# A fused attention and channel-mix kernel: the attention of the next batch issued between the matmul groups of the channel mix

## The chip, the cores and the metric

The kernel runs on one core of one Trainium2 chip. The core has five engines with a queue each: PE (matmuls and transposes, results into PSUM), ACT (activation functions), DVE (elementwise work), POOL and SP (here they mostly issue DMAs). An engine takes its own instructions in order and waits on semaphores for the others. The metric is the device time of one execution in microseconds (us), lower is better.

## The reference

Two stages, cut to what matters:

```python
# stage 1, per batch b and head h: B=8, H=8, S=576 tokens, D=64, M=32 memory slots
a   = softmax(phi, over the S tokens)          # [S, M]
k_m = a.T @ k ;  v_m = a.T @ v                 # [M, D] each
attn = softmax(q @ k_m.T / 8, over M)          # [S, M]
x[b, s, h*64:(h+1)*64] = attn @ v_m
# stage 2, on x [B, S, 512]; x_prev is x shifted by one token (0 for the first)
xk = mu_k*x + (1-mu_k)*x_prev ;  xr = mu_r*x + (1-mu_r)*x_prev
k  = maximum(xk @ w_k, 0)                      # [.., 1024]
out = sigmoid(xr @ w_r) * ((k*k) @ w_v)        # [B, S, 512], float32
```

All inputs and the output are float32; the kernel multiplies in bf16.

## The kernel before

Channels lie on the 128 partitions and tokens on the free axis in stage 2, so stage 1 has to leave x transposed (`xT`, `xk_T`, `xr_T`, each 128 x 4 x 4608).

Stage 1 is a loop over the eight batches (L90). A batch is cut into five token blocks of 128 (the last has 64). For each block, SP loads phi and POOL loads k, v and q with a cast to bf16 (L96, L102, L106, L156), one row of 64 values per token and head. ACT takes exp(phi) (L99). PE forms k_m (`psA`, L114), v_m for all pairs of heads (`psB`, L121) and the sums of exp(phi) (`psZ`, L126). DVE copies the blocks that are wanted out of PSUM (L136, L137, L148). PE transposes q (L161), DVE copies it out (L166). Then, for each of four pairs of heads, scores (`psc`, L170), exp on ACT (L175), the sums over M by a matmul with ones (`pzs`, L177), one over them as exp(-ln(z)) in two activations (L182, L183), the values (`pno`, L185) and their product with the reciprocal (L189). The three PSUM tiles of a pair share one buffer ("bigp"). DVE then makes the token difference and the two mixes (L194 to L201).

Stage 2 is a loop over nine chunks of 512 tokens (L209). Per chunk: eight groups of four matmuls for k (`pk`, L216), relu on ACT (L221) and square on DVE (L222); then, for each 128 tokens, eight matmuls (`pv`, L227), four (`pr`, L233), a sigmoid on ACT (L238), a product on DVE (L240) and the store by SP (L241). `pk`, `pv` and `pr` share two PSUM buffers ("mp"). A chunk is 80 matmuls of 512 columns.

The code writes stage 1 in full and then stage 2. The tile framework's scheduler sets the order on each engine, and it starts chunks of stage 2 as soon as their batches are there.

## Time and profile before

| | us |
|---|---|
| median of 3 runs | 418.77 |
| lowest and highest run | 416.33, 421.94 |
| span of the profiled execution, first to last instruction | 414.4 |
| busy in the span: PE, weight loads, DVE, ACT, POOL | 295.0, 118.8, 187.6, 270.4, 103.8 |
| 1392 matmuls, 505 DVE, 400 ACT instructions (table loads among them) | |
| DMA: 158471 packets, 31.23 MB written, of them 151792 under 512 bytes | |

For the profiled execution the span is the time that the profile gives; its own time with what lies around the span is not listed, and the three runs are 1.9 to 7.5 us above the span, the median 4.4 us.

How to read it: busy time is counted per engine, and the engines work beside each other. A matmul's busy time includes its way through the array, so matmuls in a row overlap; the cost of one in a row is the distance from start to start. "Granted clock" is the share of TensorE's 2.4 GHz that it was given: 1.00 is 2.4 GHz, 0.50 is 1.2 GHz; before the first record of the clock the views print 1.00, whatever it was.

### The profile page before, as it was taken

The numbers are of one execution on the slowest core, as the hardware profiler recorded it, in microseconds if no ns is written. First come the engines' busy times: TensorE is split into PE (matmuls) and PEld (weight loads), VectorE is DVE, ScalarE is ACT, GpSimd is POOL, SyncE is SP. The second block draws the span as 40 slices with busy tenths as digits, with TensorE's granted clock in tenths as the row PEclk, the third lists the DMA queues.
The fourth block names the chain that finished last, engine by engine and source line by source line (L and its number), as shares of the span: only waits on it lengthen the run. The fifth ranks groups of instructions, "written<-read, shape, count | busy, mean of one in ns | idle before, by whom it ended". The sixth has DMA issues, their size and how long they took to land.

```text
span 414.4 us, 4288 instructions
## 1 busy us (share of the span) xinstructions
PE 295.0 (71%) x1392; PEld 118.8 (29%) x1392; DVE 187.6 (45%) x505; ACT 270.4 (65%) x400; POOL 103.8 (25%) x129
## 2 busy tenths in 40 slices
PE   0055957876867698776877587467677888888884
PEld 0021322322232243323333232122223333333331
DVE  1004165647463666555756356564544232323231
ACT  1030487599998798999888888878994242423331
POOL 7244762560540263164053021010000000000000
PEclk9999999989896968878896999678898999999999
DMA  7999999892992399299289045130000101020101
GB/s 110 194 145 153 126 133 73 58 156 15 114 164 29 43 123 115 52 114 128 13 78 101 25 71 34 13 44 25 27 25 25 76 27 76 25 78 26 76 27 76
DMA packets 158471, 31.23 MB, mean 75 GB/s; under 512 B 151792, under 2 KB 153328, under 8 KB 158448
## 3 DMA queue, kind: packets, MB, share of 16 engines
q0 software_dynamic: 114608, 16.79, 59.3%
q1 hardware_dynamic: 43840, 14.17, 17.2%
q8 instruction: 11, 0.18, 0.2%
q14 instruction: 12, 0.10, 0.1%
HBM read 38.28 MB, written 9.44 MB: 115 GB/s over the span
## 4 chain that ended last, share of the span: by engine, by line
PE 30%; ACT 28%; issue 18%; DMA 15%; DVE 5%; POOL 4%; POOLq 0%; ACTq 0%; DVEq 0%
PE pv L227 11%; PE pk L216 8%; DMA kt<-in_k_dram 6%; PE pr L233 5%; DMA qt<-in_q_dram 5%; ACT L182 4%; ACT rsb L238 4%; DMA vot<-in_v_dram 4%; ACT L183 4%; ACT zsb L183 3%; ACT zsb L182 3%; ACT L238 2%; ACT esc L175 2%; DVE xT L189 2%; ACT L175 2%
## 5 line engine op out<-in xcount | busy, mean ns | idle before, releaser
L227 PE MATMUL pv<-wv,sqT 128*128 128x512 bf16 x288 | 79.8, 415 | 16.0 <-ACT rsb L238 16.0
L216 PE MATMUL pk<-xkT,wk 128*128 128x512 bf16 x288 | 79.4, 410 | 10.9 <-ACT rsb L238 5.4
L156 POOL DMA_DIRECT2D qt<-in_q_dram x40 | 33.6, 841 | 126.4 <-PE pqT L161 105.3
L189 DVE TENSOR_TENSOR xT<-pno,zsb 128x576 bf16<-128x576 f32 x32 | 24.2, 758 | 71.8 <-ACT zsb L183 64.5
L221 ACT ACTIVATE relu<-pk 128x512 bf16<-128x512 f32 x72 | 41.4, 591 | 23.0 <-PE pk L216 19.9
L238 ACT ACTIVATE rsb<-pr 128x512 f32<-128x512 f32 x36 | 21.5, 597 | 53.5 <-PE pr L233 53.4
L240 DVE TENSOR_TENSOR osb<-rsb,pv 128x512 f32<-128x512 f32 x36 | 24.6, 683 | 65.9 <-ACT rsb L238 64.8
L227 PEld LDWEIGHTS <-sqT 128*128 128x128 bf16 x288 | 29.3, 104 | 56.4 <-issue 30.7
L233 PE MATMUL pr<-wr,xrT 128*128 128x512 bf16 x144 | 42.5, 399 | 3.2 <-ACT relu L221 3.2
L175 ACT ACTIVATE esc<-psc,rZ1s 64x576 bf16<-64x576 f32 x32 | 23.5, 733 | 29.9 <-PE psc L172 29.7
L102 POOL DMA_DIRECT2D kt<-in_k_dram x40 | 34.1, 857 | 33.0 <-PE psA L114 24.0
L182 ACT ACT_TABLE_LOAD x32 | 41.1, 1283 | 0.6
L216 PEld LDWEIGHTS <-wk 128*128 128x128 bf16 x288 | 26.6, 101 | 43.9 <-issue 22.8
L222 DVE TENSOR_TENSOR sqT<-relu 128x512 bf16<-128x512 bf16 x72 | 29.6, 421 | 19.9 <-ACT relu L221 19.8
L106 POOL DMA_DIRECT2D vot<-in_v_dram x40 | 33.8, 850 | 12.4 <-PE psZ L126 5.0
L121 PE MATMUL psB<-vot,ephi 128*128 128x512 bf16 (+1 forms) x80 | 31.1, 498 | 5.8 <-DMA vot<-in_v_dram 5.2
L183 ACT ACT_TABLE_LOAD x26 | 33.4, 1283 | 0.5
L99 ACT ACTIVATE ephi<-phit 128x256 bf16<-128x256 f32 (+1 forms) x40 | 15.4, 409 | 27.6 <-DMA phit<-in_phi_dram 25.1
L170 PE MATMUL psc<-qTb,kmT 128*64 128x512 bf16 x32 | 15.2, 476 | 17.7 <-DVE xT L189 17.6
L114 PE MATMUL psA<-ephi,kt 128*128 128x128 bf16 (+1 forms) x160 | 20.5, 278 | 9.8 <-DMA kt<-in_k_dram 5.2
L197 DVE SCALAR_TENSOR_TENSOR xkT<-diff,mk,xT 128x576 bf16<-128x576 bf16 x32 | 25.9, 808 | 0.4
L201 DVE SCALAR_TENSOR_TENSOR xrT<-diff,mr,xT 128x576 bf16<-128x576 bf16 x32 | 25.9, 810 | 0.0
(48 smaller groups left out, 318.0 us busy)
## 6 DMA issues: line engine op xcount, KB each, us to landing
out_dram<-osb SPq DMA_DIRECT2D x36, 256.0 KB, 2.0
kt<-in_k_dram POOLq DMA_DIRECT2D x32, 128.0 KB, 5.6
vot<-in_v_dram POOLq DMA_DIRECT2D x32, 128.0 KB, 5.8
phit<-in_phi_dram SPq DMA_DIRECT2D x32, 128.0 KB, 5.7
qt<-in_q_dram POOLq DMA_DIRECT2D x32, 128.0 KB, 3.4
wk<-in_moe_w_k_dram POOLq DMA_DIRECT2D x1, 1024.0 KB, 9.2
wv<-in_moe_w_v_dram POOLq DMA_DIRECT2D x1, 1024.0 KB, 13.3
wr<-in_moe_w_r_dram POOLq DMA_DIRECT2D x1, 512.0 KB, 15.2
```

What stands on the lines that cost most here:

```text
L102: nc.gpsimd.dma_start(out=kt[:sn, :, :], in_=k[b, :, s0:s0 + sn, :].rearrange("h s d -> s h d"))
L106: nc.gpsimd.dma_start(out=vot[:sn, :H * D].rearrange("p (h d) -> p h d", h=H), in_=v[b, :, s0:s0 + sn, :].rearrange("h s d -> s h d"))
L156: nc.gpsimd.dma_start(out=qt[:sn, :, :], in_=q[b, :, s0:s0 + sn, :].rearrange("h s d -> s h d"))
L175: nc.scalar.activation(e_sc, psc, AF.Exp, scale=rZ1s[:, j:j + 1])
L182: nc.scalar.activation(zs_sb, pzs, AF.Ln)
L183: nc.scalar.activation(zs_sb, zs_sb, AF.Exp, scale=-1.0)
L189: nc.vector.tensor_mul(xT[:, j, b * S:(b + 1) * S], pno, zs_sb)
L216: nc.tensor.matmul(pk, lhsT=wk_sb[:, di, fi * 128:(fi + 1) * 128], rhs=xk_T[:, di, tok_sl], start=(di == 0), stop=(di == ND - 1))
L221: nc.scalar.activation(relu_t, pk[:, :], AF.Relu)
L227: nc.tensor.matmul(pv, lhsT=sq_T[:, fi, tsub * 128:(tsub + 1) * 128], rhs=wv_sb[:, fi, :], start=(fi == 0), stop=(fi == NF - 1))
L233: nc.tensor.matmul(pr, lhsT=xr_T[:, di, t0:t0 + 128], rhs=wr_sb[:, di, :], start=(di == 0), stop=(di == ND - 1))
L238: nc.scalar.activation(r_sb, pr[:, :], AF.Sigmoid)
```

## The change

The kernel is written anew around the same matmuls of stage 2. Stage 1 of batch b+1 becomes a list of steps, each with a slot number; a chunk of stage 2 has 16 slots (eight `key`, then `gate` and `value` mixed), and the program issues slot after slot, first the stage-2 group, then the steps of that slot. The scheduler is off (`manual_schedule`), so this order is the order on every engine. Steps of batch 0, and the first ones of batch 1, come ahead of slot 0.

Other parts: a batch's first 512 tokens are loaded as four tokens per partition (one run of 256 values of a head where there were four of 64) and the last 64 apart, two batches ahead; token columns are kept in that order through stage 2, and `store` puts rows back. k_m and v_m of a pair of heads come from one matmul with 64 weight columns and 256 moving columns, times a mask that clears the cross terms. The denominators are 48 rows of 96 columns for the whole batch (`zsum`), inverted by one reciprocal on DVE, split in two bf16 parts and spread again by matmuls (`spread`). exp of ln is gone. The gate is 0.5 + 0.5 tanh(x/2), with the 0.5 folded into w_v; the +1 is in the last product. All stage-1 PSUM tiles share three buffers ("at"); `pk` has two, `pr` and `pv` share three.

The diff, cut; the lines taken away are those of the loops listed above:

```diff
+NB = 4
+TAIL = 512
...
+    ctx.enter_context(tc.manual_schedule())
+    const = ctx.enter_context(tc.sbuf_pool(name="const", bufs=1))
+    big = ctx.enter_context(tc.sbuf_pool(name="big", bufs=1))
+    ld = ctx.enter_context(tc.sbuf_pool(name="ld", bufs=2))
+    work = ctx.enter_context(tc.sbuf_pool(name="work", bufs=2))
+    psum = ctx.enter_context(tc.psum_pool(name="psum", bufs=1))
...
+    def load_kv(b):
+        kvm = ld.tile([128, 2, H, NB, D], BF16, name="kvm", tag="kvm")
+        kvt = ld.tile([NT, 2, H, D], BF16, name="kvt", tag="kvt")
+        for i, t in enumerate((k, v)):
+            nc.gpsimd.dma_start(
+                out=kvm[:, i].rearrange("p h j d -> p h (j d)"),
+                in_=t[b, :, 0:TAIL, :].rearrange("h (p j) d -> p h (j d)", j=NB))
+            nc.gpsimd.dma_start(out=kvt[:, i], in_=t[b, :, TAIL:S, :].rearrange("h s d -> s h d"))
+        loads[b].update(kvm=kvm, kvt=kvt)
...
+    load_phi(0)
+    load_kv(0)
+    load_q(0)
+    mu2 = const.tile([2 * ND, 128], F32, name="mu2")
+    nc.sync.dma_start(out=mu2[:ND, :], in_=moe_mu_k.rearrange("(a b) -> a b", b=128))
+    nc.sync.dma_start(out=mu2[ND:2 * ND, :], in_=moe_mu_r.rearrange("(a b) -> a b", b=128))
+    load_phi(1)
+    wk_sb = big.tile([128, ND, Dff], BF16, name="wk")
+    wv_sb = big.tile([128, NF, Dm], BF16, name="wv")
+    wr_sb = big.tile([128, ND, Dm], BF16, name="wr")
+    nc.gpsimd.dma_start(out=wk_sb, in_=moe_w_k.rearrange("(do di) f -> di do f", di=128))
+    nc.gpsimd.dma_start(out=wr_sb, in_=moe_w_r.rearrange("(do di) d2 -> di do d2", di=128))
+    nc.gpsimd.dma_start(out=wv_sb, in_=moe_w_v.rearrange("(fo fi) d -> fi fo d", fi=128))
+    load_kv(1)
+    load_q(1)
+    identity = const.tile([128, 128], BF16, name="identity")
+    make_identity(nc, identity)
...
+        def exp_phi():
+            em = work.tile([128, NB, H, M], BF16, name="em", tag="em")
+            et = work.tile([NT, H, M], BF16, name="et", tag="et")
+            nc.scalar.activation(em.rearrange("p j h m -> p h j m"), L["phm"], AF.Exp)
+            nc.scalar.activation(et, L["pht"], AF.Exp)
+            st["em"] = em.rearrange("p j h m -> p j (h m)")
+            st["et"] = et.rearrange("p h m -> p (h m)")
+            if b + 2 < B:
+                load_phi(b + 2)
+                for j in blocks:
+                    last = j == NB
+                    n = NT if last else 128
+                    for c in range(2):
+                        for what in range(2):
+                            for jj in range(2):
+                                pr = 2 * c + jj
+                                e = st["et"][:, pr * 64:(pr + 1) * 64] if last else \
+                                    st["em"][:, j, pr * 64:(pr + 1) * 64]
+                                if what == 0:
+                                    rhs = L["kvt"][:, :, 2 * pr:2 * pr + 2, :] if last else \
+                                        L["kvm"][:, :, 2 * pr:2 * pr + 2, j, :]
+                                    o = st["kvps"][jj * 64:(jj + 1) * 64, c, :]
+                                else:
+                                    rhs = ones[:n, :]
+                                    o = st["zps"][jj * 64:(jj + 1) * 64, c:c + 1]
+                                nc.tensor.matmul(o, lhsT=e, rhs=rhs,
+                                                 start=(j == 0 and c == 0), stop=last,
+                                                 skip_group_check=True)
...
+        def norm_kv():
+            rz = work.tile([128, 2], F32, name="rz", tag="rz")
+            nc.vector.reciprocal(rz, st["zps"])
+            kvbd = work.tile([128, 2, 2, 2 * D], BF16, name="kvbd", tag="kvbd")
+            for c in range(2):
+                nc.vector.scalar_tensor_tensor(
+                    kvbd[:, c].rearrange("p a b -> p (a b)"), in0=st["kvps"][:, c, :],
+                    scalar=rz[:, c:c + 1], in1=mask.rearrange("p a h d -> p (a h d)"),
+                    op0=AL.mult, op1=AL.mult)
+            st["kvbd"] = kvbd
...
+        def tr_q(pr):
+            def go():
+                if "qT" not in st:
+                    st["qT"] = work.tile([128, NPAIR, S], BF16, name="qT", tag="qT")
+                ps = psum.tile([128, S], BF16, name="qtps", tag="at", bufs=3)
+                for j in range(NB):
+                    for i in range(2):
+                        nc.tensor.matmul(ps[i * D:(i + 1) * D, j * 128:(j + 1) * 128],
+                                         lhsT=L["qm"][:, 2 * pr + i, j, :], rhs=identity,
+                                         is_transpose=True, start=True, stop=True,
+                                         skip_group_check=True)
+                nc.tensor.matmul(ps[:, TAIL:S],
+                                 lhsT=L["qt"][:, 2 * pr:2 * pr + 2, :].rearrange("p h d -> p (h d)"),
+                                 rhs=identity[:NT, :NT], is_transpose=True, start=True, stop=True,
+                                 skip_group_check=True)
+                nc.vector.tensor_copy(st["qT"][:, pr, :], ps)
...
+        def scores(c, hf):
+            def go():
+                if "e" not in st:
+                    st["e"] = work.tile([128, 2, S], BF16, name="e", tag="e")
+                ps = psum.tile([128, HALF], F32, name="scps", tag="at", bufs=3)
+                sl = slice(hf * HALF, (hf + 1) * HALF)
+                for jj in range(2):
+                    nc.tensor.matmul(ps[jj * 64:(jj + 1) * 64, :],
+                                     lhsT=st["kmT"][:, c, jj * 64:(jj + 1) * 64],
+                                     rhs=st["qT"][:, 2 * c + jj, sl], start=True, stop=True,
+                                     skip_group_check=True)
+                nc.scalar.activation(st["e"][:, c, sl], ps, AF.Exp, scale=scale)
+            return go
+        def zsum():
+            ps = psum.tile([NROW, SEG], F32, name="zcps", tag="at", bufs=3)
+            for c in range(2):
+                for sg in range(NSEG):
+                    o = NROW - (c * 4 * NSEG + sg)
+                    nc.tensor.matmul(ps, lhsT=selz[:, o:o + NROW],
+                                     rhs=st["e"][:, c, sg * SEG:(sg + 1) * SEG],
+                                     start=(c == 0 and sg == 0), stop=(c == 1 and sg == NSEG - 1))
+            rzf = work.tile([NROW, SEG], F32, name="rzf", tag="rzf")
+            nc.vector.reciprocal(rzf, ps)
+            rhl = rhl2[b % 2]
+            nc.vector.tensor_copy(rhl[:NROW, :], rzf)
+            nc.vector.tensor_sub(rhl[LO:KR, :], rzf, rhl[:NROW, :])
+            st["rhl"] = rhl
+                n = HALF // SEG
+                for i in range(n):
+                    sg = hf * n + i
+                    nc.tensor.matmul(ps[:, i * SEG:(i + 1) * SEG],
+                                     lhsT=selb[:, c, sg].rearrange("p g m -> p (g m)"),
+                                     rhs=st["rhl"], start=(i == 0), stop=(i == n - 1),
+                                     skip_group_check=True)
+                sl = slice(hf * HALF, (hf + 1) * HALF)
+                nc.vector.tensor_mul(st["at"][:, c, sl], st["e"][:, c, sl], ps)
...
+                pss = [psum.tile([128, HALF], F32, name="nops", tag="at", bufs=3) for _ in range(2)]
+                for jj in range(2):
+                    r = slice(jj * 64, (jj + 1) * 64)
+                    nc.tensor.matmul(pss[jj], lhsT=st["kvbd"][r, c, 1, :],
+                                     rhs=st["at"][r, c, sl], start=True, stop=True,
+                                     skip_group_check=True)
+                for jj in range(2):
+                    nc.scalar.copy(st["x"][:, 2 * c + jj, sl], pss[jj])
...
+        def diff():
+            x = st["x"]
+            d = work.tile([128, ND, S], BF16, name="diff", tag="diff")
+            nc.vector.tensor_sub(d[:, :, 128:TAIL], x[:, :, 128:TAIL], x[:, :, 0:TAIL - 128])
+            nc.vector.tensor_sub(d[:, :, 1:128], x[:, :, 1:128], x[:, :, TAIL - 128:TAIL - 1])
+            nc.vector.tensor_copy(d[:, :, 0:1], x[:, :, 0:1])
+            nc.vector.tensor_sub(d[:, :, TAIL:S], x[:, :, TAIL:S], x[:, :, TAIL - 1:S - 1])
+            st["d"] = d
...
+        return [
+            (-9, exp_phi),
+            (-6, kv((0, 1))), (-5, kv((2, 3))), (-4, kv((4,))), (-4, norm_kv),
+            (-3, tr_q(0)), (-3, tr_q(1)), (-2, tr_k), (-1, tr_q(2)), (-1, tr_q(3)),
+            (0, scores(0, 0)), (1, scores(0, 1)), (2, scores(1, 0)), (3, scores(1, 1)),
+            (4, zsum),
+            (5, spread(0, 0)), (5, spread(0, 1)), (6, spread(1, 0)), (6, spread(1, 1)),
+            (7, values(0, 0)), (7, values(0, 1)), (8, values(1, 0)), (8, values(1, 1)),
+            (9, diff),
+            (10, mix(0, 0)), (10, mix(1, 0)), (11, mix(2, 0)), (11, mix(3, 0)),
+            (12, mix(0, 1)), (13, mix(1, 1)), (13, mix(2, 1)), (14, mix(3, 1)),
+        ]
...
+                nc.scalar.activation(th, pr, AF.Tanh, scale=0.5)
...
+                nc.vector.scalar_tensor_tensor(o, in0=st["pr"][ts], scalar=1.0, in1=pv,
+                                               op0=AL.add, op1=AL.mult)
...
+        return [key(fi) for fi in range(NF)] + [
+            gate(0), gate(1), value(0), gate(2), value(1), gate(3), value(2), value(3)]
...
+    slots = {}
+    for b in range(B):
+        base = 16 * (b - 1)
+        for rel in range(-9, 16):
+            slots.setdefault(base + rel, []).append((b, rel))
+    last = 16 * NCH
+    for s in range(-25, last):
+        mixing = channel_mix(s // 16) if s >= 0 and s % 16 == 0 else None
+        if mixing:
+            work_at["m"] = mixing
+        if s == 0:
+            nc.vector.tensor_scalar_mul(wv_sb.rearrange("p a b -> p (a b)"),
+                                        wv_sb.rearrange("p a b -> p (a b)"), 0.5)
+        if s >= 0:
+            work_at["m"][s % 16]()
+        for b, rel in slots.get(s, []):
+            for r, step in steps_of(b):
+                if r == rel:
+                    step()
```

POOL's queue at its start, before (a DMA row names its tile and the input, with what it waits for; the masks.py rows build the 128x128 identity that transposes need):

```order
masks.py:197 MEMSET identity 128x128
L74 DMA wk<-in_moe_w_k_dram 128x4x1024
masks.py:199 ISA
masks.py:199 AFFINE_SELECT identity<-identity 128x128 [waits Pool_49]
L75 DMA wv<-in_moe_w_v_dram 128x8x512
L76 DMA wr<-in_moe_w_r_dram 128x4x512
L102 DMA kt<-in_k_dram 128x8x64
L106 DMA vot<-in_v_dram 128x8x64
```

With the change, the same engine from the load of w_k on, which stands behind the six loads of batch 0:

```order
L102 DMA wk<-in_moe_w_k_dram 128x4x1024
L103 DMA wr<-in_moe_w_r_dram 128x4x512
L104 DMA wv<-in_moe_w_v_dram 128x8x512 [waits DMASW0_49]
L77 DMA kvm<-in_k_dram 128x8x256 [waits DMASW1_49]
L80 DMA kvt<-in_k_dram 64x8x64 [waits DMASW2_49]
L77 DMA kvm<-in_v_dram 128x8x256 [waits DMASW3_49]
L80 DMA kvt<-in_v_dram 64x8x64 [waits DMASW4_49]
L86 DMA qm<-in_q_dram 128x8x256 [waits DMASW5_49]
L89 DMA qt<-in_q_dram 64x8x64 [waits DMASW6_49]
masks.py:197 MEMSET identity 128x128
masks.py:199 ISA
masks.py:199 AFFINE_SELECT identity<-identity 128x128 [waits Pool_49]
```

The identity has moved from the head of the queue to behind all loads of two batches and the weights, and the last of these waits for an earlier load.

ACT in the middle of the kernel, before (a pair of heads of stage 1, `L182` and `L183`, with relu and sigmoid of stage 2 between):

```order
L183 ACT_TABLE_LOAD
L183 ACTIVATE zsb<-zsb 128x576
L221 ACTIVATE relu<-pk 128x512
L175 ACTIVATE esc<-psc,rZ1s 64x576
L182 ACT_TABLE_LOAD
L182 ACTIVATE zsb<-pzs 128x576
L183 ACT_TABLE_LOAD
L183 ACTIVATE zsb<-zsb 128x576
L238 ACT_TABLE_LOAD
L238 ACTIVATE rsb<-pr 128x512
L175 ACT_TABLE_LOAD
```

With the change, one period from the relu of slot 4 on (`e` is exp of the scores, `x` the copies of the attention's values, `em` and `et` the exp of the next phi, `th` the tanh of a gate):

```order
L358 ACTIVATE rl<-pk 128x512 [waits DVE_49,PE_49] x4
L292 CAST x<-nops 128x288 [waits PE_49] x4
L160 ACTIVATE em<-phm 128x8x4x32 [waits DMAHW0_49]
L161 ACTIVATE et<-pht 64x256 [waits DMAHW1_49]
L369 ACTIVATE th<-pr 128x512 [waits PE_49]
L292 CAST x<-nops 128x288 [waits PE_49] x4
L369 ACTIVATE th<-pr 128x512 [waits PE_49]
L369 ACTIVATE th<-pr 128x512 [waits DVE_49,PE_49,Activation_49]
```

The table loads between activations are gone. Four copies, the two exp of phi, a tanh and four more copies now stand in a row behind the relus of slots 4 to 7.

## Rows read from the trace of the kernel before

**Rows 1.** Stretch, length, busy us of PE, PEld, DVE, ACT, POOL; clock, DMA share, GB/s.

```profile
80.00:312.00 232.00, 168.94 (x825) 65.57 (x824) 130.62 (x348) 206.40 (x291) 63.36 (x76) 0.85 0.79 69
...
312.00:410.00 98.00, 84.89 (x372) 36.51 (x371) 29.94 (x59) 33.03 (x56) 0.00 (x0) 0.98 0.14 52
```

**Rows 2.** Groups by line, ACT: count, busy us, mean ns, idle before.

```profile
L221 ACT ACTIVATE relu<-pk 128x512 bf16<-128x512 f32 x72 | 41.4, 591 | 23.0 <-PE pk L216 19.9 <-DVE sqT L222 2.9
L182 ACT ACT_TABLE_LOAD x32 | 41.1, 1283 | 0.6
L183 ACT ACT_TABLE_LOAD x26 | 33.4, 1283 | 0.5
...
L238 ACT ACTIVATE rsb<-pr 128x512 f32<-128x512 f32 x36 | 21.5, 597 | 53.5 <-PE pr L233 53.4
...
L99 ACT ACTIVATE ephi<-phit 128x256 bf16<-128x256 f32 (+1 forms) x40 | 15.4, 409 | 27.6 <-DMA phit<-in_phi_dram 25.1 <-PE psB L121 2.3
```

**Rows 3.** Chain of waits from 325 us on: start us, us, work.

```profile
327.91 7.07 PE pk L216 x32
...
348.56 7.07 PE pk L216 x32
...
410.48 0.69 DVE osb L240
```

**Rows 4.** Busy time by stretch, as rows 1, in the loading at the start.

```profile
4.00:8.00 4.00, 0.00 (x0) 0.00 (x0) 0.00 (x0) 0.00 (x0) 4.00 (x6) 1.00 1.06 161
...
8.00:12.00 4.00, 0.00 (x0) 0.00 (x0) 0.17 (x1) 0.00 (x0) 1.41 (x2) 1.00 1.30 190
12.00:18.00 6.00, 0.00 (x0) 0.00 (x0) 0.19 (x4) 0.02 (x1) 0.87 (x1) 1.00 1.43 213
20.00:40.00 20.00, 10.05 (x51) 4.44 (x52) 4.42 (x22) 4.83 (x16) 8.39 (x10) 1.00 2.06 149
```

**Rows 5.** Timeline of PE at full clock: start us, us, instructions merged.

```profile
158.12 0.39 PE L114 MATMUL psA<-ephi,kt 128*128 128x128 bf16 x4
158.44 0.39 PE L185 MATMUL pno<-esc,vmx 64*128 64x512 bf16 x1
...
162.95 0.40 PE L170 MATMUL psc<-qTb,kmT 128*64 128x512 bf16 x1 [0.31 <-DVE xT L189]
163.19 0.19 PE L172 MATMUL psc<-qTb,kmT 128*64 128x64 bf16 x1
163.31 1.04 PE L233 MATMUL pr<-wr,xrT 128*128 128x512 bf16 x4
```

**Rows 6.** Timeline of PE, earlier in the run.

```profile
66.24 0.58 PE L170 MATMUL psc<-qTb,kmT 128*64 128x512 bf16 x1 [1.61 <-DVE xT L189]
66.62 0.26 PE L172 MATMUL psc<-qTb,kmT 128*64 128x64 bf16 x1
66.81 0.61 PE L114 MATMUL psA<-ephi,kt 128*128 128x128 bf16 x4
```

**Rows 7.** Groups by line, DVE.

```profile
L222 DVE TENSOR_TENSOR sqT<-relu 128x512 bf16<-128x512 bf16 x72 | 29.6, 421 | 19.9 <-ACT relu L221 19.8
...
L197 DVE SCALAR_TENSOR_TENSOR xkT<-diff,mk,xT 128x576 bf16<-128x576 bf16 x32 | 25.9, 808 | 0.4
L240 DVE TENSOR_TENSOR osb<-rsb,pv 128x512 f32<-128x512 f32 x36 | 24.6, 683 | 65.9 <-ACT rsb L238 64.8 <-ACT zsb L182 0.6 <-issue 0.4
L189 DVE TENSOR_TENSOR xT<-pno,zsb 128x576 bf16<-128x576 f32 x32 | 24.2, 758 | 71.8 <-ACT zsb L183 64.5 <-PE pno L187 7.3
...
L166 DVE COPY qTb<-pqT 128x512 bf16<-128x512 bf16 (+1 forms) x40 | 15.7, 393 | 17.9 <-PE pqT L161 16.4 <-PE psc L172 1.5
L194 DVE TENSOR_TENSOR diff<-xT 128x575 bf16<-128x575 bf16 x32 | 14.5, 452 | 0.3
```

**Rows 8.** Busy time by stretch, as rows 1, around one fall of the clock.

```profile
120.00:123.00 3.00, 1.67 (x8) 0.57 (x6) 2.24 (x8) 2.92 (x8) 0.26 (x1) 1.00 2.42 147
124.00:127.00 3.00, 2.29 (x9) 0.76 (x8) 0.82 (x2) 2.70 (x5) 0.00 (x0) 0.50 0.06 15
```

More of the change, by code (lines that the diff above doesn't have):

```diff
@@ new lines @@
+    load_kv(1)
+    load_q(1)
+    identity = const.tile([128, 128], BF16, name="identity")
+    make_identity(nc, identity)
+    ident_f = const.tile([2 * ND, 2 * ND], F32, name="identf")
+    nc.vector.tensor_copy(ident_f, identity[:2 * ND, :2 * ND])
+    ones = const.tile([128, 1], BF16, name="ones")
+    nc.vector.memset(ones, 1.0)
+    mask = const.tile([128, 2, 2, D], BF16, name="mask")
+    nc.vector.memset(mask, 0.0)
+    for g in range(4):
+        nc.vector.memset(mask[g * M:(g + 1) * M, :, g % 2, :], 1.0)
```

329 lines of the change are left out of this document (146 added, 183 removed).

## The prediction

> **What bounds the kernel now.** I read the busy time by stage first. From 80 to 312 us ACT is busy 206.4 of 232 us, PE 168.9, DVE 130.6 and POOL 63.4; from 312 on PE alone is full, 84.9 of 98 us [rows 1]. So there are two stages: one in which attention and channel mix are mixed and ACT is the full engine, and one of channel mix alone. The costs by line say what fills ACT: the two largest of its table-load groups are 58 loads of 1.28 us, 74.5 us [rows 2], because Exp, Ln, Exp again and Sigmoid take turns. The chain of waits then gives the pure price of stage 2. One chunk takes 20.65 us from key group to key group; its 32 key matmuls take 7.07 us, 0.221 us each [rows 3]. Eighty of them are 17.7 us; the other 3 us are waits for the two shared buffers.
>
> The start is a third stage: the transfer rate by window is 161 GB/s (written) from 4 us, 190, then 213 while the weights come, and 149 from 20 us on, when the rows of 64 values come [rows 4].
>
> **What goes.** Ln, the second Exp, Sigmoid and with them all but one table load leave ACT. What stays there per chunk is 8 relus of 0.59 us, 4 tanh of 0.60 [rows 2] and per batch four exps and eight copies of 288 columns and two exps of phi. At 0.41 us for 256 columns and 0.59 for 512 [rows 2], 288 cost 0.43, and the 1024 of the larger exp of phi 0.95. That is 7.1 + 6.5 = 13.6 us a chunk, far under PE's work below. DVE per chunk: 8 squares of 0.42, 4 last products of 0.68, 8 mixes of 0.81, the difference at 0.45 per 575 columns (1.9), copies of 0.39 to 0.47 (2.2 in all), four products of 288 columns at half of 0.76 (1.6), and an estimated 1.7 for the normalizations, small operations at these rates: 20 us [rows 7]. Also under PE. So PE should set the time from the first key group to the end, if its waits are small, and I sum its queue.
>
> **1. Ahead of the first key group: 60 us.** In the new order PE's first instruction, and DVE's, need the identity, and POOL makes it only behind the last load of batch 1, which waits for `wk`. Ahead of that land batch 0 (2.36 MB as written), the phi of batch 1 (0.59) and `wk` (1.05), 4.0 MB. From 4 to 12 us the windows give 1.4 MB [rows 4]. For the rest no row has runs of 512 bytes written. Bounds are 149 GB/s (runs of 128 bytes) and 213 (1 to 2 KB) [rows 4]; a straight line of time per run through the two, 13.7 and 96 ns per DMA engine, gives 41 ns for 512 bytes, 199 GB/s, and I take that: 12 + 2.6/0.199 = 25 us (24 to 29), and 27 with POOL's last issue and the identity itself.
>
> From there the first batch runs alone, step behind step, and PE at half clock, as before at this point: 576 columns in two matmuls take from 66.24 to 66.81, 0.57 us, where later they take 0.36 [rows 5, 6]. Twenty matmuls of 256 columns at 0.25 and twenty small ones: 6.2, to 33.5. Normalization on DVE 1.2, then transposes at 0.13 [rows 6], nine per pair of heads, held by three buffers: 38.7. Scores 8 x 0.28: 40.9. Exp, sums, reciprocal, spread and product: 44. Then eight copies of 0.43 on ACT with the exp of the next phi (1.36) among them: 49.3. Difference 1.9 and five mixes of 0.81 on DVE: 55.2. Only then DVE normalizes batch 1 (1.1), does two mixes and two copies (2.6), and PE, done with batch 1's k and v long before, can end the last two groups of transposes: 60. The loads of batch 1 (7.3 MB by then, about 42 us) lie beside this and are not late. At full clock the PE pieces would give back about 8 us.
>
> **2. A chunk with attention beside it: 31.2 us, six times.** Key, gate and value groups: 17.7. The attention steps of a batch at full clock: a matmul of 128 columns in a row costs 0.08 (four from 158.12 to 158.44) [rows 5], so 34 transposes and four short ones 3.0, and 24 of 96 columns 1.9; 20 of 256 columns at half of 0.221, 2.2; 16 of 288, 2.0; 20 of one column at an estimated 0.06 (between nothing and the 0.08), 1.2. Sum 10.3. Each visit to matmuls with 64 weight columns or rows costs some more: 576 columns from 162.95 to 163.31 are 0.36 us, 0.11 over 576 columns at the full-width rate [rows 5, 3]; 14 visits, 1.5. Upper end 11.8. The lower end is that two neighbouring 64-wide matmuls, now on different halves of the array, run side by side: half of 2.2 + 2.6 + 2.0 comes off, 8.4. The rows have 64-wide matmuls only on the first half, so none is nearer to either end; I take the middle, 10.1.
>
> The Trainium skill (TensorEngine Tiling (Array Packing), section Key Properties) has a rule for each end: different tiles work in parallel, and a change of tiling mode drains the array. The drain agrees with the 0.11 us of the row; the parallel part no row shows, and by it the sum would be that of the lower end.
>
> Then the waits. Behind key group 7, ACT has in a row a relu, four copies, two exp of phi, a tanh and four copies: 0.59 + 1.72 + 1.36 + 0.60 + 1.72 = 6.0 us [rows 2]. PE has two gate groups and eight value matmuls in that stretch, 2.8 us, and its value matmuls need buffers that these copies free: it waits 3.1. The reciprocals for `spread` come about 0.3 late. So 17.7 + 10.1 + 3.4 = 31.2, 187 us for six.
>
> **3. The rest.** Chunk 6 has only the second half of a batch beside it, and no exp of phi: 17.7 + 4.2 + 1.9 = 23.8. Chunks 7 and 8 have nothing beside them, and with three buffers for `pr` and `pv` no wait: 35.4. After the last value group follow a product of 0.69 and the store; before, 414.4 minus 410.48 is 3.9 [rows 3]: 4.0 with the hand-over.
>
> The loads of later batches (2.36 MB in 31 us) and the stores in smaller pieces lie beside this: the start moves more than twice that rate. Scaling `w_v` once on DVE (3 to 6 us by the rates of rows 7) lies beside the first key groups, whose buffers give it four relus' time. These cost nothing; without that cover the second is at most 6 us, once.
>
> **4. The clock.** Half clock follows stretches in which PE was little busy: 1.67 of 3 us from 120, then 0.50 from 124 [rows 8]. The new wait of step 2 makes one such stretch per chunk. If every second one is followed by a stretch at half clock like that in rows 8, 3 us at least, in which PE does half, it loses 0.75 us a chunk, 5 in all.
>
> Sum: 60 + 187 + 24 + 35 + 4 + 5 = 315 to 316 for the span, against 414.4. The runs' median is 4.4 above the span of before; with the same beside it **320 us**.
>
> **Rivals.**
> - *The pairs run side by side and the clock holds.* For it: the weights are put on both halves. Minus 11 and minus 5: **304**. Chance 0.25.
> - *The clock is granted as in the mixed stage of before*, 0.85 there [rows 1]. The interleaved PE work, about 189 us without waits, would lose 33 instead of 5: **348**. For it: stage 1's matmuls are short and thin here too. Against: PE was busy 73% of that stage, and would be near 88%. Chance 0.20.
> - *DVE's chain between copies and transposes sets the period.* Slots 0 to 7 of PE (10.5), ACT's 6.0, then difference, mixes, normalization, copies and last products one behind the other (14.5) and the last transposes (2.5) are 33.5 a chunk: **335**. Against: key groups and part of the gates run beside it. Chance 0.09.
> - *Slower than before: PE at half clock through the whole interleaved stage.* It loses 189 instead of 5: **504**. It decides from the point where 59% of that work (112 us lost) runs at half clock; the mean of 0.85 in rows 1 means that before it was under a fifth. Chance 0.03.
> - *The table loads do not go* (tanh and exp in different tables): at most 72 loads of 1.28, 92 us on an ACT with 200 us to spare, felt in the row of step 2 as two loads, 2.6 us a chunk: **338**. But the program of the changed kernel has one load. Chance 0.01.
>
> **How the numbers follow.** The forecast has 0.42; alone it would range from 306 to 338 (start 57 to 65, waits of 2 to 5 us a chunk). With the rivals at 304, 335 and 348 and the bounds of the start (8 us less at full clock, 5 more at 149 GB/s) the range is 292 to 362. About 2% (410 and 427) is what measurement can tell from no change. All cases but one lie under 410: faster 0.96; the half-clock case is spread over its degrees, 0.02 for within 2% and 0.02 for slower.
>
> **What would show it.** One table load; DVE's first instruction near 27 us; the first key group near 60; key group to key group 31 us for six chunks, with ACT's row of copies as the releaser of PE's waits on `nops`; 17.7 us for the last chunks; 64-wide pairs starting together or 0.11 apart; the granted clock of 60 to 275 us over 0.9. It would be wrong if PE waited for DVE or for loads in mid-kernel, or if the first key group came 15 us earlier or later.

## The result and the profile after

| | us |
|---|---|
| changed kernel, median of 4 runs | 293.61 (291.07 to 294.89) |
| kernel before, 4 runs on the same chip | 419.28 (416.33 to 421.94) |
| ratio, 95% interval | 0.7001 [0.6949, 0.7054]: faster |
| profiled execution of the changed kernel: its time, its span | 294.89, 293.1 |

Forecast 320 (292 to 362); the median lies 1.6 us inside the lower end. The profiled execution is the longest of the four; their spans go from 289.3 to 293.1, each 1.8 us below its time.

The chain of waits of the changed kernel gives the start of each chunk (start us, us, work). It answers to [rows 3].

```profile
54.31 1.82 PE pk L354 x4
...
84.60 0.97 PE pk L354 x4
...
114.71 0.97 PE pk L354 x4
...
143.16 0.97 PE pk L354 x4
...
253.61 6.91 PE pk L354 x32
270.88 6.91 PE pk L354 x32
...
288.24 0.69 DVE o L380
```

Key group to key group: 30.1 us, then 28.45, and 17.27 for the chunks with nothing beside them. The first key group comes at 54.3.

Busy time by stretch, columns as [rows 1]: the loading, a chunk with a fall of the clock, one without, and the last two chunks.

```profile
4.00:28.00 24.00, 0.41 (x3) 0.36 (x5) 0.48 (x5) 1.36 (x2) 9.65 (x14) 1.00 1.36 204
...
84.60:114.70 30.10, 27.82 (x199) 11.95 (x200) 18.55 (x40) 11.84 (x26) 4.70 (x6) 0.94 0.70 110
114.70:143.20 28.50, 26.21 (x200) 11.60 (x200) 17.93 (x39) 11.85 (x26) 4.70 (x6) 1.00 0.79 125
...
253.60:288.00 34.40, 34.40 (x161) 15.47 (x158) 13.07 (x26) 14.34 (x24) 0.00 (x0) 1.00 0.21 61
```

In the chunk without a fall (third row) PE is busy 26.2 of 28.5 us, ACT 11.9, DVE 17.9. Before, in the mixed stage, ACT was the full engine at 206 of 232 [rows 1]; now PE is, and its queue is what a chunk costs. The loads move at 204 GB/s in the loading stretch; [rows 4] gave 149 for short runs and 213 for long ones.

The groups by line, ACT (answers to [rows 2]), show where its time went.

```profile
L358 ACT ACTIVATE rl<-pk 128x512 bf16<-128x512 f32 x72 | 43.0, 597 | 88.1 <-PE pk L354 88.1
L369 ACT ACTIVATE th<-pr 128x512 f32<-128x512 f32 x36 | 21.5, 596 | 56.5 <-PE pr L366 53.7 <-DVE o L380 2.8
L292 ACT CAST x<-nops 128x288 bf16<-128x288 f32 x64 | 20.8, 413 | 3.8 <-PE nops L288 3.7
...
L160 ACT ACT_TABLE_LOAD x1 | 1.3, 1283 | 0.7 <-PEq L431 0.7
```

One table load is left. Relu and gate cost what they did.

### The profile page after: what moved, and what is told of

Its sections match the earlier page's. It is cut to its first block, busy times and chain, and to the rows that moved or that the text cites. A ratio compares the mean times of both kernels' runs of the same rounds, so it can differ in the third digit from the quotient of the medians.

```text
span 293.1 us, 4271 instructions
## 1 busy us (share of the span) xinstructions
PE 237.4 (81%) x1665; PEld 107.7 (37%) x1665; DVE 160.3 (55%) x351; ACT 104.1 (36%) x221; POOL 41.8 (14%) x57
## 4 chain that ended last, share of the span: by engine, by line
PE 68%; ACT 11%; DVE 9%; DMA 7%; POOL 2%; issue 1%; DVEq 0%; POOLq 0%
PE pv L377 22%; PE pk L354 21%; PE pr L366 10%; DMA wk<-in_moe_w_k_dram 7%; PE qtps L222 4%; ACT x L292 4%; PE kvps L188 3%; ACT rl L358 3%; PE scps L242 3%; ACT em L160 2%; DVE rzf L258 2%; PE rbps L272 2%; PE qtps L226 1%; ACT th L369 1%; DVE sq L359 1%
## 5 line engine op out<-in xcount | busy, mean ns | idle before, releaser
L358 ACT ACTIVATE rl<-pk 128x512 bf16<-128x512 f32 x72 | 43.0, 597 | 88.1 <-PE pk L354 88.1
L377 PE MATMUL pv<-wv,sq 128*128 128x512 bf16 x288 | 68.7, 385 | 0.0
L359 DVE TENSOR_TENSOR sq<-rl 128x512 bf16<-128x512 bf16 x72 | 30.6, 425 | 41.6 <-ACT rl L358 41.3
L369 ACT ACTIVATE th<-pr 128x512 f32<-128x512 f32 x36 | 21.5, 596 | 56.5 <-PE pr L366 53.7
L377 PEld LDWEIGHTS <-sq 128*128 128x128 bf16 x288 | 27.4, 99 | 32.2 <-issue 2.9
L380 DVE SCALAR_TENSOR_TENSOR o<-th,pv 128x512 f32<-128x512 f32 x36 | 24.6, 683 | 25.9 <-PE pv L377 22.3
L307 DVE SCALAR_TENSOR_TENSOR xrT<-diff,mu,x 128x576 bf16<-128x576 bf16 x32 | 25.2, 810 | 0.0
L288 PE MATMUL nops<-atn,kvbd 64*128 64x288 bf16 x64 | 15.1, 301 | 11.5 <-ACT x L292 9.6
L307 DVE SCALAR_TENSOR_TENSOR xkT<-diff,mu,x 128x576 bf16<-128x576 bf16 x32 | 24.0, 812 | 0.0
L292 ACT CAST x<-nops 128x288 bf16<-128x288 f32 x64 | 20.8, 413 | 3.8 <-PE nops L288 3.7
```

The lines of the kernel that those rows point to most:

```text
L288: nc.tensor.matmul(pss[jj], lhsT=st["kvbd"][r, c, 1, :], rhs=st["at"][r, c, sl], start=True, stop=True, skip_group_check=True)
L292: nc.scalar.copy(st["x"][:, 2 * c + jj, sl], pss[jj])
L307: nc.vector.scalar_tensor_tensor(dst[:, d4, b * S:(b + 1) * S], in0=st["d"][:, d4, :], scalar=mu1[:, which * ND + d4:which * ND + d4 + 1], ...
L358: nc.scalar.activation(rl, pk, AF.Relu)
L359: nc.vector.tensor_mul(st["sq"][:, fi, :], rl, rl)
L369: nc.scalar.activation(th, pr, AF.Tanh, scale=0.5)
```

## The experiments

Each ratio is to the kernel before, with its 95% interval. "The changed kernel" is the one above, whose lines the diffs start from, unless said otherwise.

### Do the two column halves run side by side?

**Program order of the pairs.** In `kv` and `tr_q` all matmuls of one half are written ahead of those of the other, where they alternated.

```diff
-                        for what in range(2):
-                            for jj in range(2):
+                        for jj in range(2):
+                            for what in range(2):
...
-                for j in range(NB):
-                    for i in range(2):
+                for i in range(2):
+                    for j in range(NB):
```

> The changed kernel with another order of the same matmuls: in the k/v step and in the transposes of q, the matmuls of one 64-column half follow one another and no longer alternate with those of the other half. Theory (the two halves of the array work side by side): in the changed kernel eight transposes of 128 columns start within 0.35 us and a pair of 256 columns plus a pair of one column takes 0.14 to 0.16; apart, a batch's k/v step goes from 1.6 to about 2.8 us and its transposes from 1.9 to 2.5 or 3, so six chunks grow by 1.7 to 2.4 us each and the first two batches, at half clock, by some 3 in all on the path: 305 to 312 us. Rival (the small price comes from the narrow weights alone, whatever the neighbour): 292 to 296 us, and the same start-to-start times.

Measured: 294.92, ratio 0.7038 [0.7000, 0.7076]; the changed kernel's 0.7001 lies in that interval. Expected were 305 to 312 if the halves run side by side, so this looked like evidence against it, and I read PE's timeline. The changed kernel:

```profile
103.61 0.30 PE L188 MATMUL kvps<-kvm,em 128*64 128x256 bf16 x2
103.74 0.17 PE L188 MATMUL zps<-ones,em 128*64 128x1 bf16 x2
103.77 0.28 PE L188 MATMUL kvps<-kvm,em 128*64 128x256 bf16 x2
...
109.06 0.41 PE L222 MATMUL qtps<-identity,qm 128*64 128x128 bf16 x8
109.41 0.20 PE L226 MATMUL qtps<-identity,qt 64*128 64x64 bf16 x1
```

And the reordered one, at the same step:

```profile
102.18 0.30 PE L188 MATMUL kvps<-kvm,em 128*64 128x256 bf16 x2
102.31 0.17 PE L188 MATMUL zps<-ones,em 128*64 128x1 bf16 x2
```

Both show the two halves' `kvps` together, then both `zps`. In the reordered program the order as written, with the scheduler off, is `kvps`, `zps` of one half and then `kvps`, `zps` of the other; single records start at 102.178 and 102.185 (`kvps`), 102.312 and 102.318 (`zps`). So the second `kvps` started 0.13 us ahead of a `zps` that stands before it in the program. The edit had not taken the pairs apart, and its result says nothing against them.

The Trainium skill (PSUM — Partial Sum Buffer, section Engine vs sequencer instructions) says that matmuls start and complete in program order. These records do not agree for matmuls on different column halves.

**A fence between the halves.** Half by half as above, with a matmul of one column over the full width ahead of each half; the tail's transpose, also of full width, stands between the halves of `tr_q`.

```diff
+                for jj in range(2):
+                    nc.tensor.matmul(st["zps"][:, 2:3], lhsT=identity, rhs=ones,
+                                     start=(jj == 0 and 0 in blocks), stop=False,
+                                     skip_group_check=True)
+                    for j in blocks:
...
+                    if i == 0:
+                        nc.tensor.matmul(ps[:, TAIL:S],
...
```

> The changed kernel with the two 64-column halves kept apart by a matmul of full width between them: in each k/v step all of one half, a one-column matmul with 128 weight columns, then all of the other half (five such fences more per batch than needed for the result); in the transposes of q the tail transpose, which has 128 weight columns, now stands between the halves. The run before this one only changed the order and the halves still started within 13 ns of each other. Theory (halves run side by side, and PE takes the other half's matmuls ahead of program order unless something of full width stands between): a batch's k/v step goes from 1.6 to 2.8 us or more and its transposes from 1.9 to 2.4 to 2.8 us, 1.7 to 2.3 us a chunk, at half clock twice that in the start: 304 to 311 us. Rival (narrow weights are cheap in themselves): at most the six fences a batch, 294 to 297 us.

Measured: 315.50, ratio 0.7507 [0.7466, 0.7549]. The same step in PE's timeline:

```profile
110.70 0.30 PE L191 MATMUL kvps<-kvm,em 128*64 128x256 bf16 x1
110.83 0.17 PE L191 MATMUL zps<-ones,em 128*64 128x1 bf16 x1
110.86 0.28 PE L191 MATMUL kvps<-kvm,em 128*64 128x256 bf16 x1
...
118.15 0.41 PE L225 MATMUL qtps<-identity,qm 128*64 128x128 bf16 x4
118.49 0.20 PE L230 MATMUL qtps<-identity,qt 64*128 64x64 bf16 x1
118.62 0.42 PE L225 MATMUL qtps<-identity,qm 128*64 128x128 bf16 x8
```

Four matmuls now come where eight did (`x4` from 118.15 to 118.49, against `x8` from 109.06 to 109.41): the side-by-side reading is shown. The last row shows the same within the run: between the tail transposes of two groups no fence stands, and there the second half of one group and the first half of the next, eight in all, again take 0.36 us. Per batch the k/v step takes 3.96 us where it took 1.70, two groups of transposes 1.30 instead of 0.96; a fence costs 0.10 of it, six times. The undisturbed chunk grew from 28.45 to 31.15. So 0.6 of the 2.7 us a chunk are the fences themselves. The run is 4.5 us above what was expected: a chunk grew by 2.7 where 1.7 to 2.3 was said, and the first key group comes 5.1 later (59.4), since the first batch's steps lie bare on the path. The two matmuls of a score step start together too (single records at 115.610 and 115.613 in the changed kernel), but what scores and values gain from it was not tried.

### ACT's row

**exp of phi one slot later,** behind the second four copies instead of between the two fours.

```diff
-            (-9, exp_phi),
+            (-8, exp_phi),
```

> The changed kernel with the two exp of the next batch's phi one slot later, behind the last four copies of the attention's values instead of ahead of the tanh of gate 0. Theory (ACT's row of relu, copies, exp and tanh is what PE waits for at the last value matmul, 1.3 us a chunk): the wait shrinks to about 0.5, the half-clock stretches behind it go, the first batch's chain loses 1.4 us of exp: 284 to 288 us, granted clock above 0.99. Rival (the wait only moves to the k/v step, which then waits for the exp, or to DVE's difference): 292 to 294 us.

Measured: 286.65, ratio 0.6843 [0.6805, 0.6881]. The changed kernel's ACT, one row of it:

```profile
95.70 1.30 ACT L292 CAST x<-nops 128x288 bf16<-128x288 f32 x4
96.85 1.10 ACT L160 ACTIVATE em<-phm 128x1024 bf16<-128x1024 f32 x1
97.81 0.42 ACT L161 ACTIVATE et<-pht 64x256 bf16<-64x256 f32 x1
98.11 0.59 ACT L369 ACTIVATE th<-pr 128x512 f32<-128x512 f32 x1
98.59 1.28 ACT L292 CAST x<-nops 128x288 bf16<-128x288 f32 x4
```

From the first copy to the last end it is 4.17 us. PE goes on before that end, when the first of the second four copies has freed a buffer:

```profile
99.04 0.28 PE L288 MATMUL nops<-atn,kvbd 64*128 64x288 bf16 x1 [1.30 <-ACT x L292]
```

PE's waits in the changed kernel (us in all, times, longest):

```profile
PE nops L288 <- ACT x L292: 9.6, 8, 1.3
PE rbps L272 <- DVE rhl L261: 6.6, 8, 1.4
...
PE nops L288 <- DVE atn L277: 1.1, 7, 0.2
```

and with the later exp:

```profile
PE nops L288 <- ACT x L292: 4.4, 7, 0.6
```

The wait on the copies halves, 1.30 to 0.62 a chunk, the period falls to 27.77, and the first key group comes 1.2 earlier. No stretch at half clock is left in mid-kernel. In the changed kernel the two falls begin at 99.2 and 157.3 us, within 0.4 of the end of this wait (99.0 and 157.6). They differ between executions: the mean clock of its four is 0.984 to 0.999, and 0.996 to 0.997 in the four with the later exp. Its windows around one fall, and at the same place of the next chunk:

```profile
96.00:99.00 3.00, 1.74 (x9) 0.43 (x9) 0.26 (x1) 3.00 (x9) 0.00 (x0) 1.00 0.02 5
99.00:102.00 3.00, 2.96 (x8) 1.04 (x8) 1.57 (x4) 1.47 (x4) 0.00 (x0) 0.54 0.73 195
126.10:129.10 3.00, 1.75 (x9) 0.45 (x9) 0.28 (x1) 3.00 (x9) 0.00 (x0) 1.00 0.00 0
```

PE was as little busy in the third stretch as in the first, and the clock held behind it. Why one fell and the other not stays open.

**Sigmoid again,** as a plain product and without the scaling of `w_v`; everything else as changed.

```diff
-                nc.scalar.activation(th, pr, AF.Tanh, scale=0.5)
+                nc.scalar.activation(th, pr, AF.Sigmoid)
...
-                nc.vector.scalar_tensor_tensor(o, in0=st["pr"][ts], scalar=1.0, in1=pv,
-                                               op0=AL.add, op1=AL.mult)
+                nc.vector.tensor_mul(o, st["pr"][ts], pv)
```

> The changed kernel with Sigmoid in place of Tanh, a plain product and no scaling of w_v: ACT then loads a table twice a chunk, 14 loads of 1.28 us instead of one. Theory (in the new order a load costs only where ACT's row is waited for: ahead of the first gate, inside the wait on the copies): 1.3 us in each of six chunks, some of it again as clock falls: 300 to 306 us. Rival (every load is on the path): 13 x 1.28, 310 us or more; other rival (ACT has room everywhere): 293 to 296.

Measured: 317.46, ratio 0.7556 [0.7511, 0.7601]; the time is the rival's, but not for its reason. From its waits, its ACT timeline and its windows:

```profile
PE nops L288 <- ACT x L292: 19.0, 8, 2.7
...
PE pk L354 <- ACT rl L358: 1.4, 6, 0.2
```

```profile
102.07 1.28 ACT L369 ACT_TABLE_LOAD   x1
```

```profile
121.00:152.80 31.80, 27.86 (x199) 12.03 (x199) 18.45 (x39) 14.45 (x28) 4.70 (x6) 0.95 0.67 107
```

Fourteen loads make 18.0 us, and the kernel is 23.9 longer. Two a chunk: one in the row, where PE's wait grows from 1.30 to 2.73, and one ahead of the first exp of the scores, where PE waits only 0.23. So one load of the two is on the path, as the theory had it, and PE waits 1.66 a chunk more. The rest is the clock, which the theory had too small: the chunks, 31.8 to 33.0 us, are 3.3 to 4.5 longer than 28.45, at a clock of 0.90 to 0.95.

### The start

**Identity early.** POOL makes it behind the loads of k and v of batch 0.

```diff
     load_kv(0)
+    identity = const.tile([128, 128], BF16, name="identity")
+    make_identity(nc, identity)
...
-    identity = const.tile([128, 128], BF16, name="identity")
-    make_identity(nc, identity)
```

> The changed kernel with the identity made behind the k and v loads of batch 0 instead of behind all loads. Theory (the identity's place in POOL's queue holds PE and DVE until 27.4 us): PE starts when batch 0's k and v are there (about 16.6 us), its transposes when q is there (about 21); from the first transpose to the first key group are 22.8 us in the changed kernel, so the first key group comes near 44 instead of 54.2: 283 to 285 us. Rival (the start is bound by the transfers of batch 1, whose last load lands near 36 to 38): first key group at 46 to 50, 288 to 290. If neither queue nor transfers matter: 293.6.

Measured: 289.64, ratio 0.6919 [0.6872, 0.6967]: the rival. The first batch's k/v matmuls start at 16.3 instead of 27.8, and then PE waits for the loads of the second, in its timeline:

```profile
41.61 0.42 PE L188 MATMUL kvps<-kvm,em 128*64 128x256 bf16 x2 [8.50 <-DMA kvm<-in_v_dram]
```

Of 11.5 us gained, 5.2 arrive at the first key group (49.1).

**Short runs.** Each large load of k, v and q as four, of 64 values a run.

```diff
-            nc.gpsimd.dma_start(
-                out=kvm[:, i].rearrange("p h j d -> p h (j d)"),
-                in_=t[b, :, 0:TAIL, :].rearrange("h (p j) d -> p h (j d)", j=NB))
+            for j in range(NB):
+                nc.gpsimd.dma_start(
+                    out=kvm[:, i, :, j, :],
+                    in_=t[b, :, 0:TAIL, :].rearrange("h (p j) d -> p h j d", j=NB)[:, :, j, :])
...
```

> The changed kernel with its main k, v and q loads cut into four DMAs each, one per token of a partition, so that a run is 64 values again (same place in SBUF, same order of everything else). Theory (short runs cost in the start alone): the loads ahead of the identity move at about 149 instead of 199 GB/s and POOL issues 33 DMAs before it, identity at 31 to 34 instead of 27: 297 to 302 us; in mid-kernel 15 DMAs of 0.85 us lie beside a chunk of 28.5. Rival (loads of later batches come late too): 310 us and more. Other rival (run length does not matter): 293 to 295.

Measured: 310.72, ratio 0.7448 [0.7398, 0.7499], as slow as the rival, but not for its reason. Its waits, and its chain:

```profile
DVE identf L114 <- POOL identity masks.py:199: 43.4, 1, 43.4
...
POOL kvm L78 <- DMA wv<-in_moe_w_v_dram: 4.3, 1, 4.3
```

```profile
19.37 15.80 DMA wv<-in_moe_w_v_dram
...
70.83 1.82 PE pk L356 x4
```

All of it is at the start: the identity 16.0 us later, the first key group 16.5. From there undisturbed chunks take 28.45 as before, with no load among PE's waits. POOL's loads of batch 1 now wait until `wv` has landed, and the identity stands behind them. I had counted the lower rate and not the DMAs that POOL waits through, 15 a batch instead of 6. The rate is the smaller part: from 4 to 28 us this run moves 184 GB/s where the changed kernel moves 204, and for the 4.9 MB of that stretch this makes 2.6 us, an estimate from these two rates. The other 13 fit POOL's waiting, which was not tried alone.

### What the gain is made of

**Attention not interleaved.** In the changed kernel each batch's steps all come in the last slot of the chunk before it is needed.

```diff
-            slots.setdefault(base + rel, []).append((b, rel))
+            slots.setdefault(base + rel if base + rel < 0 else 16 * b - 1 if b else -1, []).append((b, rel))
```

> The changed kernel with the same steps in another order: all attention steps of batch b stand behind the last group of chunk b-1 instead of between its groups (batch 0 and the first steps of batch 1 as in the change). Theory (attention is a chain of short steps over PE, ACT and DVE that only the key, gate and value groups fill): each of six batches then takes the 20 us that batch 0 takes from its first k/v matmul to its last key mix in the changed kernel, less where the clock is full, beside 17.3 us of groups: 37 a chunk against 28.5, and clock falls: 340 to 365 us. Rival (interleaving hides little, PE's own work is what costs): under 305 us.

Measured: 340.38, ratio 0.8104 [0.8053, 0.8154].

```profile
120.40:155.60 35.20, 29.01 (x198) 13.73 (x198) 19.08 (x40) 12.51 (x26) 4.70 (x6) 0.84 0.61 98
```

A chunk takes 35 us; PE is idle 6.2 of it (2.3 with interleaving), and the clock is 0.84.

**One table in the kernel before.** Copy for Ln and Tanh for Sigmoid, without the reciprocal of the denominators and the true gate.

```diff
-            nc.scalar.activation(zs_sb, pzs, AF.Ln)
+            nc.scalar.activation(zs_sb, pzs, AF.Copy)
...
-            nc.scalar.activation(r_sb, pr[:, :], AF.Sigmoid)
+            nc.scalar.activation(r_sb, pr[:, :], AF.Tanh)
```

> The kernel before with Copy in place of Ln and Tanh in place of Sigmoid, so that ACT runs the same number of activations from one table; it leaves out the reciprocal of the denominators and the true gate. Theory (before, ACT's table loads set the mixed stage): 91 loads of 1.28 us go, 117 us of ACT; the stage of 232 us in which ACT was busy 206 and PE 169 shrinks towards PE's time and its waits: 345 to 370 us. Rival (the three PSUM tiles of a pair in one buffer make the stage a chain, and the loads hide in PE's share): 395 us or more. If it came to 300, the table loads alone would be the whole gain of the change.

Measured: 381.00, ratio 0.9128 [0.9029, 0.9226], between the two expectations. Its mixed stage:

```profile
80.00:300.00 220.00, 178.70 (x904) 69.58 (x904) 138.59 (x355) 106.25 (x214) 60.08 (x73) 0.88 0.81 76
```

ACT is busy 106 of 220 us now. Yet 92 loads of 1.28 us less one, 117 us, gave back 38: a full engine was not the whole price of that stage. PE now waits 34 us for transfers of v, k and q in all (15 before), and POOL issues those of q only when PE has freed a buffer.

**The reciprocal on DVE in the kernel before,** at its full size, in place of Ln and Exp.

```diff
-            nc.scalar.activation(zs_sb, pzs, AF.Ln)
-            nc.scalar.activation(zs_sb, zs_sb, AF.Exp, scale=-1.0)
+            nc.vector.reciprocal(zs_sb, pzs)
```

> The kernel before with the reciprocal of the denominators by DVE at full size (32 times 576 columns on 128 partitions) in place of Ln and Exp. The changed kernel's reciprocal takes 0.744 us for 96 columns on 48 partitions, 7.75 ns a column. Theory (the price goes by columns): 4.4 us each, 141 us more on DVE, which then has 300 us and over and becomes the bound: 430 to 470 us, slower than before although most table loads go; so the compact form is what makes a DVE reciprocal possible. Rival (a reciprocal costs what a copy of 576 columns costs, 0.5 to 0.8): 350 to 375.

Measured: 463.99, ratio 1.1116 [1.0997, 1.1235], slower. Its DVE groups, and the groups of the changed kernel:

```profile
L182 DVE RECIPROCAL zsb<-pzs 128x576 f32<-128x576 f32 x32 | 120.1, 3754 | 18.6 <-PE pzs L179 18.3
```

```profile
L258 DVE RECIPROCAL rzf<-zcps 48x96 f32<-48x96 f32 x8 | 6.0, 744 | 2.1 <-PE zcps L254 2.1
```

DVE is now the fullest engine, busy 220 of the 260 us from 80 to 340. At 6.5 to 7.8 ns a column, 576 columns cost five times the product of that size (0.758, [rows 7]). Compact denominators are thus what makes the DVE reciprocal affordable: 6 us instead of 120.

### Versions that go further

**Identity early and exp of phi later together.**

> Identity early and exp of phi one slot later together. If both gains are real and lie in different places they add: 293.6 - 9 - 7, 276 to 280 us. If the loads of batch 1 bound the start once the identity is early, the start's part is smaller: 281 to 284.

Measured: 281.78, ratio 0.6727 [0.6684, 0.6770]: the two gains, 4.0 and 7.0 us, add up to 11.8 within the runs' spread. The start's part is the smaller one, as in the second expectation.

**Start and slots.** The loads of batch 1 stand ahead of `w_r` and `w_v`; the steps are spread anew; `w_v` is scaled at slot 7.

```diff
+    identity = const.tile([128, 128], BF16, name="identity")
+    make_identity(nc, identity)
...
+    load_kv(1)
+    load_q(1)
     nc.gpsimd.dma_start(out=wr_sb, in_=moe_w_r.rearrange("(do di) d2 -> di do d2", di=128))
     nc.gpsimd.dma_start(out=wv_sb, in_=moe_w_v.rearrange("(fo fi) d -> fi fo d", fi=128))
-    load_kv(1)
-    load_q(1)
...
-            (-9, exp_phi),
+            (-11, exp_phi),
...
-            (0, scores(0, 0)), (1, scores(0, 1)), (2, scores(1, 0)), (3, scores(1, 1)),
-            (4, zsum),
+            (0, scores(0, 0)), (1, scores(0, 1)), (1, scores(1, 0)), (2, scores(1, 1)),
+            (3, zsum),
...
-            (7, values(0, 0)), (7, values(0, 1)), (8, values(1, 0)), (8, values(1, 1)),
+            (7, values(0, 0)), (7, values(0, 1)), (8, values(1, 0)), (9, values(1, 1)),
...
-        if s == 0:
+        if s == 7:
```

> A version built from the findings: identity early; loads of k, v and q of batch 1 ahead of w_r and w_v; scaling of w_v at slot 7; exp of phi in slot 5, where ACT has room; scores in slots 0, 1, 1, 2 and the sums in slot 3, so that the reciprocal has two key groups of cover; the last value pair in slot 9. Expected against 281.8 us of the version with identity and exp of phi alone: the wait of 0.74 us on the reciprocal and 0.6 on the copies go, 1.3 us in each of seven chunks, 9; the start gains up to 6 since batch 1 lands some 8 us earlier: 266 to 273 us. Rival: the start stays bound by the transfers (first key group not before 47 us) and the waits move to DVE: 276 to 282.

Measured: **265.22**, ratio 0.6323 [0.6268, 0.6377], the best version, just under the expected 266 to 273. Its chain and a chunk of it:

```profile
41.67 1.81 PE pk L354 x4
...
68.89 0.97 PE pk L354 x4
...
95.27 0.97 PE pk L354 x4
```

```profile
68.90:95.30 26.40, 25.72 (x199) 11.61 (x200) 18.76 (x41) 12.04 (x26) 4.71 (x6) 1.00 0.89 141
```

The first key group comes 12.6 us earlier than in the changed kernel, and a chunk takes 26.38 in four of six (27.2 and 27.3 in the others), with PE busy 97%. From its first record, at 43.4, the clock reads 1.00 up to the tail. What is left ahead of the first key group are transfers: PE waits 7.9 us for the mixing weights at the very start, then 7.0 for v and 4.7 for q. Against the version before it, 8.2 us come from the start and 1.39 from a chunk; which of the moves gave how much was not tried.

## Why the prediction was right or wrong

Right in its sign, its bound and its range, 26.4 us too long in its number. That the range held, by 1.6 us, is in part luck: its ends are not sums of the terms shown (304 less the 8 us of a start at full clock is 296, not 292), and neither condition came in full: the clock fell twice, and the start ran at half clock. The terms, 315 to 316 against a span of 293.1, and what lies around it:

| term | forecast | measured | |
|---|---|---|---|
| to the first key group | 60 | 54.3 | -5.7 |
| six chunks, with the clock | 187 + 5 | 175.7 | -16.3 |
| chunk 6 | 23.8 | 23.65 | -0.1 |
| chunks 7 and 8 | 35.4 | 34.6 | -0.8 |
| tail | 4.0 | 4.9 | +0.9 |
| around the span | 4.4 | 1.8 | -2.6 |

These make -24.6; the rest is rounding and the median, 1.3 below the profiled execution.

**The start.** POOL's identity and DVE's first instruction came as forecast; DVE's timeline:

```profile
27.37 0.16 DVE L112 CAST identf<-identity 8x8 f32<-8x8 bf16 x1 [27.37 <-POOL identity masks.py:199]
```

Half clock came too: the first `kvps` are 0.27 us apart in pairs, where a later chunk has 0.14. The step of the start that failed is "Twenty matmuls of 256 columns at 0.25 and twenty small ones: 6.2". They run in pairs, and the step took 2.9 (27.8 to 30.7). The transposes ended 4.0 early, at 34.7, and the rest of the chain only added 1.7 to that.

**The chunk** of 31.2 is 28.45 undisturbed: 17.27 of groups, 2.2 of waits (0.74 on the reciprocal, 0.16 and 1.30 on `nops`) and so 8.98 of attention on PE. The groups were said to take 17.7, 0.4 more. Two more sizes failed, of 1.1 to 1.2 us a chunk each.

- "I take the middle, 10.1." The lower end, 8.4, was nearer. The pairs run side by side, as the fence shows, worth 2.1 us of chunk without the fences' own 0.6. The rows before held no pair, and the edge between the bounds had to be guessed; the rival that went with the lower end had 0.25.
- "0.59 + 1.72 + 1.36 + 0.60 + 1.72 = 6.0 us". That ACT's copies release PE on `nops` was right; the wait is 1.30 and not 3.1. I added up durations, as if instructions stood end to end. Copies in a row start 0.29 us apart, though each is listed with 0.41, and from the first copy on the row takes 4.17 where the sum gives 5.4. For PE the forecast had used starts; for ACT it did not. I also let PE wait for the whole row, where it needs only the fifth of the eight copies: it goes on 0.83 us before the row ends. And what was set against the row is wrong twice: two gate groups and eight value matmuls are 16 of 0.221, 3.5 us and not 2.8, and in the trace the second gate group and the value matmuls come behind the wait and cover none of it.

One term of the waits was off the other way: the reciprocal was said to come 0.3 late, and PE waits 0.74 for it (on DVE it takes as long itself). Scaling `w_v` takes 1.63, once, where 3 to 6 was said, and cost nothing: what the first chunk takes longer lies in its first two key groups, at half clock (2.20 and 2.06 us from start to start, with scores between, where later ones take 1.21). No load of a later batch shows among PE's waits, as forecast.

**The clock.** 5 was said, 5.0 is what the six chunks took over 6 times 28.45: 1.8 in the first, which began at half clock, and 3.1 in two falls. The place was right, behind the wait on ACT's row, as the later exp of phi showed. That 5 met 5.0 is luck: the forecast had three falls and nothing for the first chunk, and executions of the same kernel differ in their falls.

**Around the span.** The 4.4 was the median less a span from another execution. In these runs a time is its own span plus 1.8; the other 2.6 was the spread of the runs before, and belonged to no term.

**The rivals.** The one at 304, pairs side by side and a clock that holds, was right in its first half; the clock did not quite hold, 3.1 us in two falls of the profiled execution, though the one of 291.07 us has a mean clock of 0.999. The one at 348 failed: by chunk the clock was 0.94 to 1.00 from 84.6 us on. DVE's chain at 335 failed: DVE was busy 18 of 28.5 us and no chunk waited for it beyond the 0.9. The half-clock case did not come near even without interleaving (0.84). Table loads did go; with the two a chunk that sigmoid brings, 317 and not 338 is the price.

The Trainium skill (TensorEngine Tiling (Array Packing), section Key Properties) says that different tiles can work in parallel; the trace after and the fence agree, 0.14 us for two `kvps` and two `zps`, 0.14 for one of each with the fence.

**Where the 126 us went.** Table loads alone gave 38 in the kernel before. The rest of the rewrite without interleaving brings 381 to 340; pairs side by side have up to 22 of that, fences included (measured in the interleaved order). Interleaving gives 47, waits and clock together. These are steps on one path, not terms that add in any order.

## What to carry to other kernels

Count a queue by the distance from start to start, on ACT as on PE; the listed durations overlap. When a rewrite makes one engine the bound, sum that engine's queue, then look for the longest row of work on another engine that releases it: moving one step out of such a row gave 7 us here (1.2 of them in the start), and a table load in it cost more than its own length, with the clock that fell behind it. At the start, see what stands ahead of the first small thing that everybody needs, and then what is late behind it: early identity alone gave half of what it freed, because the loads of the next batch were then late; the version that moved these too, among other changes, gained 12.6 us there.

## What was unexpected of the hardware

- PE takes matmuls of the other column half ahead of program order: `kvps` of the second half started 0.13 us before a `zps` that stood ahead of it, and a matmul of full width between them stopped it. That an engine takes its own instructions in order, as said at the start of this document, does not hold for PE there.
- ACT starts copies of 288 columns 0.29 us apart, each listed with 0.41.
- DVE's reciprocal costs 6.5 to 7.8 ns a column (3.75 us for 576 on 128 partitions, 0.744 for 96 on 48).
- The clock fell behind a stretch in which PE was busy 1.74 of 3 us, and held behind one of 1.75 at the same place of the next chunk.
